# The end phases of an attention + feed-forward kernel: sums of quarters made in PSUM from one PSUM and one SBUF operand, and the seven products' chains in another order

## The chip, the cores and the metric

The kernel runs on one core of a Trainium2 chip. Its engines are named as the profile names them: PE (TensorE, matrix products; PEld is its load of stationary operands), DVE (VectorE), ACT (ScalarE), POOL (GpSimd) and SP (SyncE, which here only issues DMAs). SBUF and PSUM are the two on-chip memories; a matmul writes to PSUM, which has eight banks of 512 fp32 values in each of 128 partitions. The metric is the device time of one execution in microseconds; lower is better.

## The reference

Causal attention by blocks of 64 positions over 8 batches and 8 heads (576 positions, head size 64), then a feed-forward layer over the 4608 resulting rows. The end phases, which the change touches, compute a part of the feed-forward.

```python
scores = scale * np.matmul(q, k.transpose(0, 1, 3, 2))
...
attn = attn / (np.sum(attn, axis=-1, keepdims=True) + 1e-09)
...
x = np.ascontiguousarray(attn_out.transpose(0, 2, 1, 3)).reshape(B * S, H * D)
...
h = x @ w_in                              # 4608 x 512 by 512 x 2048
g = h * (1.0 / (1.0 + np.exp(-h)))
return (g @ w_out).astype(np.float32)     # 4608 x 2048 by 2048 x 512
```

## The kernel before

**Precision.** Each fp32 operand of the feed-forward is kept as two numbers of a format that PE takes at full rate: H, the rounded value, and L, the rest. A product then takes three matmuls (H by H, H by L, L by H). H is made by a copy on ACT, L by a subtraction "source minus H" on DVE or POOL. The helper `parts` (L857) records such a pair, `ops` (L861) records one addition or subtraction, and both end in `tt` (L848), whose only line, L849, stands in the profile for all of them.

**Main part and end phases.** Up to about 906 us the kernel does attention and, interleaved, the feed-forward of 14 of its 18 blocks of 256 rows in the plain way. Blocks 14 to 17 (`LATER`) are left for the end. They form two double blocks of 512 rows, whose rows wait in `x_dram`. Their two matrix products are done with seven products of quarters in place of eight, as Strassen and Winograd do it, which needs sums and differences of quarters of both operands ("q" below), and sums of products at the end.

**Phase b, the first product and silu.** `item` (L975) is one double block by 256 columns of `w_in`: seven products of six matmuls each. Phase b is 16 items: double block 0 with column groups d = 0 to 3, double block 1 with 0 to 3 and 4 to 7, double block 0 with 4 to 7. Products chain in PSUM: bank X takes products 1, 6, 7 and 4, each added to those before it; Z takes 5 and 3; Y takes 2. Between two links of a chain the value so far is copied to SBUF (`keep`, names s1, s2, s5, s3), since it is needed on its own; the next link may start only when that copy has read the bank. `add` makes the four quarters of the item's result from one bank and one kept value (one of the four from two kept values), ACT applies silu, and SP saves the two halves `g0` and `g1` to `g_dram`. There are two buffers of `g0`, one of `g1`.

**Preparations.** `prep_x` (L887) loads the quarters of one double block (tiles `rx`), makes four differences of them in place and splits seven quarters in H and L; it runs three times. `prep_s` (L925) makes the four sums of quarters of a column group of `w_in`, eight times, from a tile `raw` that holds the quarters' H + L again. `prep_t` (L947) does the same for a row group of `w_out`, eight times. `prep_g` (L1068) loads the saved g's quarters and makes their sums and splits, 16 times, for phase c. All differences are made in SBUF from two SBUF operands; the L's are shared out between DVE and POOL.

**Phase c, the second product.** `mult_c` (L1098) is one of four parts (q) of a block of 256 rows: seven products of six matmuls each, 16 calls in all. Each product has half a bank for the whole block; after the fourth part `keep_c`, `add_c` and `store_c` combine the seven and write the result. Successive blocks alternate between two sets of four banks.

**What sets the order.** Each step is put in a list by `at` (L833) with a planned time in us, where 0 is the start of phase b and `ITEM` = 4.94 the planned length of an item; the list is sorted by that time and issued (L1160). Planned times only order the instructions of each engine. Each engine then takes its own in that order and waits at each for what it needs.

Of the kernel before, what the change touches and what calls it, by code (L numbers as in the profile page):

```python
# [20 lines left out]
P = 128  # L21
# [22 lines left out]
USE = (1, 2, 6, 5, 7, 3, 4)  # L44
# [97 lines left out]
def attn_ffn(ctx: ExitStack, tc: tile.TileContext, qk, v, qk0, v0, qk1, v1, w_in, w_out, out):  # L142
# [694 lines left out]
    for i in range(left):  # L837
        at(FULL * (i - left), ffn, 1)
# [7 lines left out]
    right = {}  # L846

# [9 lines left out]
    def parts(t, h, l, src, eng, lag=0.9):  # L857
        at(t, lambda: A.copy(h, src()))
        at(t + lag, lambda: tt(eng, l, src(), h, SUB))

    def ops(t, e, out, a, b, op):  # L861
        at(t, lambda: tt(e, out(), a(), b(), op))

# [23 lines left out]
    def prep_x(t, u):  # L887
        z = {}

        def load(c):  # L890
            raw(z, c, "rx")
            nc.sync.dma_start(out=z[c].rearrange("p (c n) t -> p c (n t)", c=2), in_=x_dram[order[u]][:, 2 * c : 2 * c + 2, :])

        def q(c, n):
            return lambda: z[c].rearrange("p (c n) t -> p c n t", c=2)[:, :, n]

        b11, b12, b21, b22 = q(0, 0), q(0, 1), q(1, 0), q(1, 1)

        def t2():
            if u:  # L900
                z["t"] = right["p"].tile([P, 2, TB], F32, tag="tx", name="tx")
            return z["t"] if u else b22()

        def hl(t, j, src, eng):
            p = pair(u, j)
            if u:
                t = max([t] + [u * span - ITEM + (USE.index(i) + 1) * ITEM / 7 + 0.02 for i in USE if ring[u - 1][i] == ring[u][j]])
            parts(t, p[:, :, 0], p[:, :, 1], src, eng)

        at(t, load, 0)  # L910
        at(t, load, 1)
        hl(t + 4.0, 1, b11, V)
        hl(t + 4.7, 2, b21, G)
        ops(t + 5.6, V, b11, b12, b11, SUB)
        hl(t + 5.4, 3, b22, V)
        ops(t + 6.3, V, b12, b22, b12, SUB)
        ops(t + 7.0, V, t2, b22, b11, SUB)
        two_ = (lambda: z["t"]) if u else b22
        ops(t + 7.7, V, b21, b21, two_, SUB)
        hl(t + 7.7, 6, two_, G)  # L920
        hl(t + 8.4, 5, b11, V)
        hl(t + 9.1, 7, b12, G)
        hl(t + 9.8, 4, b21, V)

    def prep_s(t, d):  # L925
# [3 lines left out]
        h21, l21 = [w[:, 0:2, cols(d, 1)] for w in wi]  # L929
        at(t, raw, z, 0)  # L930

        def q(i, j=None):
            return lambda: z[0].rearrange("p q (c m) -> p q c m", c=2)[:, i : i + 1 if j is None else j]

        def whole(f):
            tt((G, V)[f], z[0][:, 2 * f : 2 * f + 2].rearrange("p q (c m) -> p (q c) m", c=2), f32(wi[0][:, :, cols(d, f)]), f32(wi[1][:, :, cols(d, f)]), ADD)

        at(t, whole, 0)
        at(t, whole, 1)
        ops(t + 0.9, V, q(3), q(2), q(3), ADD)  # L940
        ops(t + 1.4, V, q(2), q(0), q(2), SUB)
        ops(t + 1.8, V, q(0), q(3), q(0), SUB)
        ops(t + 2.3, V, q(1), q(1), q(0), SUB)
        parts(t + 1.4, h21, l21, lambda: q(3)()[:, 0], V, 1.6)
        parts(t + 2.8, H, L, q(0, 3), G)

    def prep_t(t, d):  # L947
# [3 lines left out]
        B = [w[:, 2 * d : 2 * d + 2, :].rearrange("p f (n m) -> p (f n) m", n=2) for w in wo]  # L951
        at(t, raw, z, 0)

        def q(i, j=None):
            return lambda: z[0][:, i : i + 1 if j is None else j]

        at(t, lambda: tt(G, z[0], f32(B[0]), f32(B[1]), ADD))
        ops(t + 2.6, V, q(0), q(1), q(0), SUB)
        ops(t + 3.0, V, q(1), q(3), q(1), SUB)
        ops(t + 3.5, V, q(3), q(3), q(0), SUB)  # L960
        ops(t + 3.9, V, q(2), q(2), q(3), SUB)
        parts(t + 3.5, H[:, 0:2], L[:, 0:2], q(0, 2), V)
        parts(t + 4.4, H[:, 2:4], L[:, 2:4], q(2, 4), G)
# [11 lines left out]
    def item(t, u, d, k):  # L975
        z = {}
        e = d % HALFD
        stat = {
            1: [w[:, 0:2, cols(d, 0)] for w in wi],
            2: [w[:, 2:4, cols(d, 0)] for w in wi],  # L980
            4: [w[:, 2:4, cols(d, 1)] for w in wi],
            5: [w[:, 0:2, cols(d, 1)] for w in wi],
            6: [w[:, e, 0] for w in sv],
            3: [w[:, e, 1] for w in sv],
            7: [w[:, e, 2] for w in sv],
        }

        def prod(i, o):
            if i == 1:
                z["X"] = bank(k % 2)[:, :TB]  # L990
                z["g"] = [both(k) for k in range(2)]
            elif i == 2:
                z["Y"] = bank(2)[:, :TB]
            elif i == 5:
                z["Z"] = pU.tile([P, 512], F32, tag="U", name="Z")[:, :TB]
            x = pair(u, i)
            n = 0
            for c in range(2):
                for a, b in ((0, 0), (0, 1), (1, 0)):
                    nc.tensor.matmul(z[o], stat[i][a][:, c], x[:, c, b, :], start=i in (1, 2, 5) and n == 0, stop=n == 5, skip_group_check=True)  # L1000
                    n += 1

        def keep(e, name, o):
            z[name] = half("s1" if name == "s5" else name)
            (e.copy if e is A else e.tensor_copy)(z[name], z[o])

        def add(e, q, a, b):
            tt(e, z["g"][q[0]][:, q[1]], z[a], z[b], ADD)

        def silu2(h):  # L1010
# [10 lines left out]
        p = ITEM / 7  # L1021
        for n, (i, o) in enumerate(((1, "X"), (2, "Y"), (6, "X"), (5, "Z"), (7, "X"), (3, "Z"), (4, "X"))):
            at(t + n * p, prod, i, o)
        at(t + p + 0.01, keep, A, "s1", "X")
        at(t + 2 * p + 0.01, add, V, (0, 0), "Y", "s1")
        at(t + 2.6 * p, silu2, 0)
# [5 lines left out]
        at(t + 6 * p + 0.45, silu2, 1)  # L1032
        at(t + 7 * p + 0.1, save, 1)
        at(t + 7 * p + 0.15, silu21)
        at(t + 7 * p + 0.5, save, 0)

    at(-0.005, start_b)
    for u in range(nuse):
        if u == 0 or order[u] != order[u - 1]:
            prep_x(u * span - 14.0, u)  # L1040
        for e in range(HALFD):
            d = e + HALFD * (u >= NDBL)
            t = u * span + e * ITEM
            if u in (0, NDBL):
                prep_s(t - 6.5 - (u > 0) * 1.5, d)
            item(t, u, d, u * HALFD + e)
    for d in range(HALFD):
        prep_t(end_b - span - 13.0 + 6.0 * d, d)
        prep_t(end_b - span + 11.0 + 5.5 * d, HALFD + d)

    flat = lambda z: z.rearrange("p a b c -> p (a b c)")
    et = lambda z: z.rearrange("p (j e t) -> p j e t", e=2, t=P)
# [15 lines left out]
    def prep_g(t, blk, q, c, tag):  # L1068
# [12 lines left out]
        def w(i, j=None):  # L1081
            return lambda: z[0].rearrange("p q (e t) -> p q e t", e=2)[:, i : i + 1 if j is None else j]
# [121 lines left out]
```

## Time and profile before

| what | us |
|---|---|
| median of the two runs | 1151.69 |
| the two runs | 1150.3 and 1153.09 |
| the profiled execution, its own time | 1154.32 |
| its span, first to last instruction | 1152.6 |
| PE busy in the span | 1057.3 (92%) |
| DVE busy | 948.2 (82%) |
| POOL busy | 829.2 (72%) |
| ACT busy | 793.9 (69%) |

The profile is of one execution. Its times count from the start of its span, and busy shares are means over parts with different limits. A row of a group of instructions reads: line, engine, operation, output <- inputs by the names in the program, partitions x elements, type, and how many; behind the first bar the busy time in all (us) and the mean of one (ns); behind the second the time that the engine sat idle just before them and what ended most of it ("<-ACT s L1005" is ACT's instruction of line 1005 that wrote s). A row of the timeline gives start (us), length (us), engine, instruction and, in brackets, the idle time before it and what ended it. L1000 is PE in phase b, L1111 PE in phase c.

### The profile page before, as it was taken

The page shows a single profiled execution, that of the slowest core. Times are in us where ns is not written, and L with a number is a line of the kernel's source. Part 1 is how long each engine was busy: PE and PEld are TensorE (multiplying, and loading weights), DVE is VectorE, ACT ScalarE, POOL GpSimd, SP SyncE. Part 2 cuts the span into 40 slices and gives each one's busy share as a digit, 9 for nine tenths or more (in the row PEclk, how much of TensorE's full clock was granted, in tenths as well). Part 3 has the DMA queues.
Part 4 walks back from the last instruction along what each step waited for, and adds up shares of the span by engine and source line. Part 5 has one row for each costly group of instructions (what it writes and reads, how often), then busy time and mean ns, then how long its engine had stood idle before and what let it go on. Part 6 is the DMA issues. An engine that isn't in the chain of part 4 may idle for free.

```text
span 1152.6 us, 21493 instructions
## 1 busy us (share of the span) xinstructions
PE 1057.3 (92%) x7348; PEld 966.5 (84%) x7348; DVE 948.2 (82%) x2513; ACT 793.9 (69%) x1294; POOL 829.2 (72%) x751
## 2 busy tenths in 40 slices
PE   9999999999989997999999779999999787677987
PEld 8888999999978886889989669889889687577887
DVE  7986799999699996999985789999992757879665
ACT  5776688889788877888884768888873454443332
POOL 5766699889969886798976678878773646655344
PEclk9999999999999998999999889999999899788999
DMA  7873333232232321313221222332312033132431
GB/s 272 274 251 107 80 82 82 59 82 59 63 91 49 90 57 41 90 49 92 67 73 45 55 71 66 84 88 58 99 46 64 22 124 107 48 121 66 119 92 56
DMA packets 61389, 102.06 MB, mean 89 GB/s; under 512 B 7264, under 2 KB 34400, under 8 KB 61280
## 3 DMA queue, kind: packets, MB, share of 16 engines
q1 hardware_dynamic: 61280, 100.69, 30.9%
q8 instruction: 58, 0.95, 0.3%
q14 instruction: 51, 0.42, 0.1%
HBM read 80.74 MB, written 19.92 MB: 87 GB/s over the span
## 4 chain that ended last, share of the span: by engine, by line
PE 45%; DVE 28%; issue 8%; ACT 7%; POOL 7%; DMA 4%; SPq 2%; POOLq 0%; DVEq 0%; ACTq 0%
PE h L652 15%; PE o L687 15%; PE U L405 5%; PE S L326 4%; DVE Mx L270 3%; DVE Dx L270 3%; DVE raw L849 3%; PE S L1000 2%; DVE rx L849 2%; DVE m L341 1%; DVE Xm L279 1%; DVE xu L416 1%; ACT p L367 1%; POOL pl L381 1%; DVE MR L274 1%
## 5 line engine op out<-in xcount | busy, mean ns | idle before, releaser
L652 PE MATMUL h<-x,wi 128*128 128x256 f32 x2688 | 349.5, 284 | 0.0
L652 PEld LDWEIGHTS h<-x,wi 128*128 128x128 f32 x2688 | 339.8, 191 | 8.5 <-issue 0.5
L687 PE MATMUL o<-wo,g 128*128 128x512 f32 x1296 | 328.9, 399 | 0.0
L381 POOL TENSOR_TENSOR pl<-p,ph 128x448 fp32r<-128x448 f32 (+1 forms) x192 | 225.7, 1202 | 86.6 <-ACT ph L373 86.5
L687 PEld LDWEIGHTS o<-wo,g 128*128 128x128 f32 x1296 | 238.5, 190 | 48.6 <-issue 0.7
L670 POOL TENSOR_TENSOR g<-g,g 128x512 fp32r<-128x512 f32 x112 | 145.4, 1298 | 57.9 <-ACT g L665 42.7
L270 DVE TRANSPOSE_TENSOR_REDUCE Mx<-S 64x4 f32<-64x128 f32 (+4 forms) x384 | 132.9, 401 | 57.2 <-PE S L326 57.0
L270 DVE TRANSPOSE_TENSOR_REDUCE Dx<-p 128x14 f32<-128x448 f32 (+3 forms) x320 | 122.5, 445 | 0.1
L367 ACT ACTIVATE p<-T 128x512 f32<-128x512 f32 (+1 forms) x192 | 106.9, 605 | 19.7 <-POOL ph L383 14.0
L405 PE MATMUL U<-ph,vc 128*128 128x448 f32 (+3 forms) x320 | 78.8, 312 | 34.4 <-DVE xu L421 22.3
L302 POOL TENSOR_TENSOR qh<-qkraw,qh 64x576 fp32r<-64x576 f32 x64 | 91.7, 1433 | 18.0 <-ACT qh L298 9.1
L373 ACT CAST ph<-p 128x512 fp32r<-128x512 f32 (+1 forms) x192 | 104.0, 596 | 0.7 <-PE U L405 0.5
L659 ACT ACTIVATE g<-h 128x512 f32<-128x512 f32 x112 | 67.0, 598 | 47.4 <-POOL g L670 31.6
L367 ACT ACT_TABLE_LOAD x60 | 77.0, 1283 | 28.1 <-DVE T L356 26.8
L405 PEld LDWEIGHTS U<-ph,vc 128*128 128x128 f32 x320 | 59.1, 196 | 44.0 <-POOL ph L383 27.9
L326 PE MATMUL S<-qh 128*128 128x448 f32 (+3 forms) x320 | 91.1, 297 | 1.0 <-DVE T L356 0.7
L665 ACT CAST g<-g 128x512 fp32r<-128x512 f32 x112 | 69.4, 620 | 22.2 <-PE o L687 20.2
L326 PE MATMUL S<-ql,qh 128*128 128x448 f32 (+3 forms) x320 | 83.8, 306 | 0.0
L659 ACT ACT_TABLE_LOAD x64 | 82.1, 1283 | 1.1
L298 ACT CAST qh<-qkraw 128x1024 fp32r<-128x1024 f32 x64 | 66.8, 1044 | 16.8 <-DMA qkraw<-in_qk_dram 13.4
L304 POOL TENSOR_TENSOR ql<-qkraw,qh 128x448 fp32r<-128x448 f32 x64 | 74.1, 1158 | 5.0
L358 DVE TENSOR_TENSOR T<-S,MR 128x256 f32<-128x256 f32 (+2 forms) x192 | 72.9, 405 | 0.0
(206 smaller groups left out, 1959.5 us busy)
## 6 DMA issues: line engine op xcount, KB each, us to landing
qkraw<-in_qk_dram SPq DMA_DIRECT2D x128, 256.0 KB, 3.9
vraw<-in_v_dram SPq DMA_DIRECT2D x64, 160.0 KB, 3.0
gd<-g SPq DMA_DIRECT2D x32, 256.0 KB, 2.1
wst<-in_moe_w_out_dram SPq DMA_DIRECT2D x15, 512.0 KB, 5.0
rx<-gd SPq DMA_DIRECT2D x44, 128.0 KB, 2.7
wst<-in_moe_w_in_dram SPq DMA_DIRECT2D x10, 512.0 KB, 5.2
out_dram<-ot SPq DMA_DIRECT2D x17, 256.0 KB, 2.9
v<-in_v_dram SPq DMA_DIRECT2D x12, 256.0 KB, 5.9
```

Of the source, the lines that this page charges most:

```text
L270: nc.vector.tensor_reduce(out=out, in_=in_, axis=AX.X, op=op, apply_transpose=True)
L302: nc.gpsimd.tensor_tensor(out=u.qh[64:, NQ:], in0=u.raw[64:, NQ:], in1=u.qh[64:, NQ:], op=ALU.subtract)
L304: nc.gpsimd.tensor_tensor(out=u.ql, in0=u.raw[:, :NQ], in1=u.qh[:, :NQ], op=ALU.subtract)
L326: nc.tensor.matmul(u.ps(c, w, m), u.kk[:, j * P : j * P + m], qq[:, q0 : q0 + w], start=i == 0, stop=i == 1)
L367: nc.scalar.activation(u.p[:, c:e], T[:, c:e], AF.Exp, scale=SCALE)
L373: nc.scalar.copy(u.ph[:, c:e], u.p[:, c:e])
L381: nc.gpsimd.tensor_tensor(out=u.pl[:, c:e], in0=u.p[:, c:e], in1=u.ph[:, c:e], op=ALU.subtract)
L405: nc.tensor.matmul(U[:m, q0 : q0 + w], u.vc[:, j, :m], (u.ph, u.pl)[pp][:, c : c + w], start=n == 0, stop=n == 8)
L652: nc.tensor.matmul(h[:, f, :], wi[wt][:, c, w], x[:, xt, :], start=n == 0, stop=n == 3 * CT - 1)
L659: nc.scalar.activation(g, hs.pop((blk, d)), AF.Silu)
L670: nc.gpsimd.tensor_tensor(out=g2[:, 1], in0=g, in1=g2[:, 0], op=ALU.subtract)
L687: nc.tensor.matmul(o, g2[:, gt, f, tk], wo[wt][:, 2 * d + f, c], start=d == 0 and n == 0, stop=d == NSTEP - 1 and n == 5,)
```

## The change

The sums of quarters are no longer made in SBUF. A new helper `quad` copies one quarter into PSUM with ACT and makes all four sums there, each from one operand in PSUM and one in SBUF; H and L are then made from PSUM, all these L's by DVE. `prep_x` does the same with 512-element quarters. Only L's of unchanged quarters stay on POOL, which also makes both halves of `prep_s`'s `raw`. Banks for these sums come from the two tags (`h` and `o`) that phase c no longer uses, since each of its blocks now takes the same four banks; a small table `held` pushes a preparation's planned time back until its buffers are free by the plan.

In an item the products now come in the order 6, 5, 2, 7, 1, 3, 4, where the 1 is the next item's. s3 is gone: the result that needed it is read from X before product 4 is added. s5 is copied by ACT, and all four adds are on DVE. In phase c the seven products are combined in another pairing, by seven adds on DVE and one copy.

```diff
-USE = (1, 2, 6, 5, 7, 3, 4)
+USE = (1, 6, 5, 2, 7, 3, 4)
...
+    USED = {i: n for n, i in enumerate((6, 5, 2, 7, 1, 3, 4))}
+    p7 = ITEM / 7
...
+    def quad(t, z, q, kind, where, outs):
+        def x(i):
+            return lambda: z["b"][i // 2][:, 256 * (i % 2) : 256 * (i % 2) + 256]
+
+        def start():
+            z["b"] = psum(where)
+            A.copy(x(3)(), q(2 if kind == "S" else 1)())
+
+        t = wait(where, t)
+        hold(where, t + 3.15)
+        at(t, start)
+        if kind == "S":
+            ops(t + 0.5, V, x(0), x(3), q(3), ADD)
+            ops(t + 0.9, V, x(1), q(0), x(3), SUB)
+            ops(t + 1.3, V, x(2), x(0), q(0), SUB)
+            ops(t + 1.7, V, x(3), q(1), x(2), SUB)
...
+        for i, n, h, l, c in outs:
+            parts(t + (2.2 if i > 1 else 1.72) + 0.05 * i, h, l, lambda i=i, n=n, c=c: c(z["b"][i // 2][:, 256 * (i % 2) : 256 * (i % 2) + 256 * n]), V, 0.75)
+        return t + 3.15
...
 def prep_g
-        parts(t + 4.0, H[0][:, 0:2], L[0][:, 0:2], w(0, 2), V)
-        parts(t + 4.1, H[0][:, 2:3], L[0][:, 2:3], w(3), V, 0.7)
-        ops(t + 5.3, V, w(3), w(2), w(3), ADD)
-        ops(t + 5.7, V, w(2), w(0), w(2), SUB)
-        ops(t + 6.1, V, w(0), w(3), w(0), SUB)
-        ops(t + 6.5, V, w(1), w(1), w(0), SUB)
-        parts(t + 6.9, H[1], L[1], w(0, 4), G, 1.2)
+        parts(t + 4.5, H[0][:, 0:2], L[0][:, 0:2], lambda: z[0][:, 0:2], G, 0.7)
+        parts(t + 5.2, H[0][:, 2:3], L[0][:, 2:3], lambda: z[0][:, 3:4], G, 0.7)
+        end = quad(t + 4.0, z, lambda i: lambda: z[0][:, i], "S", where, [(0, 2, H[1][:, 0:2], L[1][:, 0:2], c), (2, 2, H[1][:, 2:4], L[1][:, 2:4], c)])
...
 def item
-        at(t + p + 0.01, keep, A, "s1", "X")
-        at(t + 2 * p + 0.01, add, V, (0, 0), "Y", "s1")
-        at(t + 3 * p + 0.01, keep, A, "s2", "X")
-        at(t + 4 * p + 0.01, keep, V, "s5", "Z")
-        at(t + 5 * p + 0.01, keep, A, "s3", "X")
-        at(t + 5.6 * p, add, G, (1, 1), "s5", "s3")
-        at(t + 6 * p + 0.01, add, V, (1, 0), "Z", "s2")
+            at(t + USED[i] * p7 - ITEM * (i == 1), prod, k, i, o)
+        at(t - 2 * p7 + 0.01, keep, "s1", "X")
+        at(t + p7 + 0.01, keep, "s2", "X")
+        at(t + 2 * p7 + 0.01, keep, "s5", "Z")
+        at(t + 3 * p7 + 0.01, add, 0, 0, "Y", "s1")
+        at(t + 4 * p7 + 0.01, add, 1, 1, "X", "s5")
+        at(t + 6 * p7 + 0.01, add, 1, 0, "Z", "s2")
...
 def mult_c
-            z["b"] = banks_c(z["n"])
+            z["b"] = [bank(0), bank(2), pU.tile([P, 512], F32, tag="U", name="c2"), bank(1)]
```

Of the new `prep_x`, `prep_s` and `prep_t`: `prep_s` and `prep_t` call `quad`, with one 256-element L each for two of the sums of `prep_s` and 512-element L's otherwise; `prep_x` makes its four differences and four L's of them as eight DVE instructions of 512 elements.

The first place is PE at the start of phase b. S is a PSUM bank (the X of one item, or Y), Z the bank of products 5 and 3; `wi`, `sv` hold the stationary operands, `x` and `xown` the moving ones. Before, from the second half of product 1 on:

```order
L1000 MATMUL S_11589<-x,wi_78 128x256 x2
L1000 MATMUL S_11589<-x,wi_79 128x256
L1000 MATMUL S_11599<-x,wi_78 128x256 x2
L1000 MATMUL S_11599<-x,wi_79 128x256
L1000 MATMUL S_11599<-x,wi_78 128x256 x2
L1000 MATMUL S_11599<-x,wi_79 128x256
L1000 MATMUL S_11589<-xown,sv_11387 128x256 x2
L1000 MATMUL S_11589<-xown,sv_11388 128x256
```

One product (2, in S_11599) stands between products 1 and 6 of the chain in S_11589. Now, on PE at the border of the first and second item, from the second half of the second item's product 1 on:

```order
L1054 MATMUL S_11652<-x,wi_78 128x256 x2
L1054 MATMUL S_11652<-x,wi_79 128x256
L1054 MATMUL Z<-x,sv_11387 128x256 x2
L1054 MATMUL Z<-x,sv_11388 128x256
L1054 MATMUL Z<-x,sv_11387 128x256 x2
L1054 MATMUL Z<-x,sv_11388 128x256
L1054 MATMUL S_11594<-x,wi_78 128x256 x2
L1054 MATMUL S_11594<-x,wi_79 128x256
L1054 MATMUL S_11594<-x,wi_78 128x256 x2
L1054 MATMUL S_11594<-x,wi_79 128x256
L1054 MATMUL S_11652<-x,sv_11387 128x256 x2
```

Two products of the item before (3 in Z, 4 in S_11594) now stand between products 1 and 6 in S_11652.

The second place is DVE between the tenth and the eleventh item of phase b, from the tenth's last add. Before (`raw`, `rx`, `tx` are SBUF tiles):

```order
L849 TENSOR_TENSOR g_12237<-Z,s_12281 128x256
L849 TENSOR_TENSOR raw<-raw 128x256 x2
L849 TENSOR_TENSOR wi_79<-raw,wi_78 128x2x128
L849 TENSOR_TENSOR raw<-raw 128x256
L849 TENSOR_TENSOR x<-rx,x 128x2x256
L849 TENSOR_TENSOR raw<-raw 128x256
L849 TENSOR_TENSOR wi_79<-raw,wi_78 128x2x256
L849 TENSOR_TENSOR g_12319<-S_12334,s_12341 128x256
```

Now, with q the sums in PSUM:

```order
L851 TENSOR_TENSOR g_12310<-Z,s_12289 128x256
L851 TENSOR_TENSOR wi_79<-q,wi_78 128x2x128
L851 TENSOR_TENSOR sv_11388<-q,sv_11387 128x256
L851 TENSOR_TENSOR x<-q,x 128x2x256
L851 TENSOR_TENSOR q<-rx,q 128x512
L851 TENSOR_TENSOR sv_11388<-q,sv_11387 128x512
L851 TENSOR_TENSOR q<-q,raw 128x256
L851 TENSOR_TENSOR q<-raw,q 128x256
L851 TENSOR_TENSOR x<-q,x 128x2x256
L851 TENSOR_TENSOR q<-raw,q 128x256
L851 TENSOR_TENSOR g_12401<-S_12384,s_12337 128x256
```

Each instruction now has one operand in PSUM, and nine in place of seven stand between the two adds.

The third place is DVE where phase c begins, from the last item's last add. Before:

```order
L849 TENSOR_TENSOR g_12715<-Z,s_12765 128x256
L849 TENSOR_TENSOR raw<-raw 128x256 x4
L849 TENSOR_TENSOR wi_79<-raw,wi_78 128x2x256
L849 TENSOR_TENSOR x<-rx,x 128x256
L849 TENSOR_TENSOR x<-rx,x 128x512
L849 TENSOR_TENSOR rx<-rx 128x256 x4
L849 TENSOR_TENSOR raw<-raw 128x256 x4
```

Now:

```order
L851 TENSOR_TENSOR g_12803<-Z,s_12777 128x256
L851 TENSOR_TENSOR sv_11387<-q,sv_11388 128x512 x2
L851 TENSOR_TENSOR q<-q,raw 128x256
L851 TENSOR_TENSOR q<-raw,q 128x256 x3
L851 TENSOR_TENSOR q<-q,rx 128x256
L851 TENSOR_TENSOR wi_79<-q,wi_78 128x2x256
L851 TENSOR_TENSOR q<-rx,q 128x256
L851 TENSOR_TENSOR q<-q,rx 128x256
L851 TENSOR_TENSOR wi_79<-q,wi_78 128x2x256
L851 TENSOR_TENSOR q<-rx,q 128x256
L851 TENSOR_TENSOR x<-q,x 128x512 x2
```

All L's of the sums now stand on DVE, among them those that POOL had before; from this add on to the end of the last `prep_t`'s and the fifth `prep_g`'s DVE work there are 38 such instructions without an add of a result between them.

More of the change, by code (lines that the diff above doesn't have):

```diff
@@ L913, in prep_x @@
[L913 to L925, printed above, removed]
+        at(t + 4.0, start)
+        hl(t + 4.2, 1, b11, G)
@@ L926, in prep_s @@
+        for _ in range(2):
+            hold("rx", max(ends) + 0.05)
+    def prep_s(t, d, where):
         z = {}
@@ L973, in both @@
         return right["p"].tile([P, 2, TB], F32, tag=f"g{k}", name=f"g{k}", bufs=2 - k)
[L975 to L988, printed above, removed]
+    items = [{} for _ in range(nuse * HALFD)]
@@ L998, in prod @@
[L998 to L1008, printed above, removed]
@@ L1010, in silu2, with item, keep, add @@
-        def silu2(h):
+        if i in (1, 2, 4, 5):
+            stat = [w[:, (0, 2)[i in (2, 4)] :, cols(d, i > 2)] for w in wi]
+        else:
+            stat = [w[:, e, {7: 0, 6: 1, 3: 2}[i]] for w in sv]
+        x = pair(u, i)
+        n = 0
+        for c in range(2):
+            for a, b in ((0, 0), (0, 1), (1, 0)):
+                nc.tensor.matmul(z[o], stat[a][:, c], x[:, c, b, :], start=i in (1, 2, 5) and n == 0, stop=n == 5, skip_group_check=True)
+                n += 1
+    def item(t, k):
+        z = items[k]
+        u, e = divmod(k, HALFD)
+        d = e + HALFD * (u >= NDBL)
+        def keep(name, o):
+            z[name] = half(name)
+            A.copy(z[name], z[o])
+        def add(h, f, a, b):
+            if "g" not in z:
+                z["g"] = [both(j) for j in range(2)]
+            tt(V, z["g"][h][:, f], z[a], z[b], ADD)
+        def silu_b(h):
@@ L1066, in attn_ffn, with prep_g @@
     blocks = [2 * dbl + h for dbl in order[NDBL:] for h in range(2)]
-    def prep_g(t, blk, q, c, tag):
+    def prep_g(t, blk, q, c, tag, where):
         H, L = c
```

194 lines of the change are left out of this document (110 added, 84 removed).

## Prediction

> **What bounds the kernel now.** I read the 40 slices first, since the change touches the end alone. Of PE's busy tenths and of the TensorE clock's, the last ten of 40 slices are the end phases.
>
> ```profile
> PE   9999999999989997999999779999999787677987
> PEclk9999999999999998999999889999999899788999
> ```
>
> Up to there PE is nearly full; in the end phases it falls to 6 to 8 tenths, and its clock falls too. So something feeds PE too slowly there. Next the start of phase b, and the busy times by stretch (columns: stretch, length; busy time and count of PE, PEld, DVE, ACT, POOL; granted clock; DMA).
>
> ```profile
> 905.98 1.23 PE L1000 MATMUL S<-x,wi 128*128 128x256 f32 x9
> ...
> 906.00:1040.00 134.00, 98.92 (x673) 94.05 (x672) 99.72 (x151) 62.38 (x144) 75.89 (x52) 0.88 0.27 91
> 1040.00:1148.80 108.80, 91.22 (x674) 87.55 (x672) 77.52 (x117) 33.13 (x58) 50.96 (x28) 0.92 0.29 83
> 1148.80:1152.60 3.80, 0.00 (x0) 0.00 (x0) 0.42 (x2) 0.00 (x0) 0.56 (x1) 1.00 0.37 138
> ```
>
> Phase b takes 134.0 us, phase c 108.8, the last store 3.8. What would they take with PE never waiting? The same product, two items apart, in an undisturbed stretch of b, and two successive parts of c:
>
> ```profile
> 947.34 0.89 PE L1000 MATMUL S<-xown,wi 128*128 128x256 f32 x6
> ...
> 957.75 0.88 PE L1000 MATMUL S<-xown,wi 128*128 128x256 f32 x6
> ...
> 1071.98 0.40 PE L1111 MATMUL S<-wo,xown 128*128 128x256 f32 x2
> ...
> 1077.02 1.60 PE L1111 MATMUL S<-wo,sv 128*128 128x256 f32 x12
> ```
>
> An item of b takes (957.75 - 947.34) / 2 = 5.2 us, a part of c 1077.02 - 1071.98 = 5.04. Sixteen of each are 83.3 and 80.6 us. So 134.0 - 83.3 = 50.7 us are lost in b and 108.8 - 80.6 = 28.2 in c, together 78.9. PE's waits (behind the colon: us in all, times, longest) say to whom:
>
> ```profile
> PE S L1000 <- ACT s L1005: 19.4, 13, 5.5
> PE Z L1000 <- DVE s L1005: 15.7, 8, 3.0
> PE c L1111 <- POOL x L849: 5.3, 4, 1.7
> PE S L1111 <- POOL x L849: 4.1, 4, 1.4
> PE c L1111 <- ACT x L858: 2.9, 1, 2.9
> PE c L1111 <- POOL sv L849: 1.8, 1, 1.8
> PE S L1111 <- POOL sv L849: 1.8, 1, 1.8
> PE c L1111 <- POOL wi L849: 0.8, 1, 0.8
> PE c L1111 <- ACT wi L858: 0.7, 1, 0.7
> ```
>
> In b it is 35.1 us for the copies that part the chains (s1, s2, s3 by ACT, s5 by DVE), in c 17.4 us for H's and L's. That is 52.5 of the 78.9. The other 26.4 are matmuls at a lower clock, 0.5 us for each us of waiting. One such wait, on all three engines:
>
> ```profile
> 975.11 2.38 POOL L849 TENSOR_TENSOR raw<-wo,wo 128x1024 f32<-128x1024 f32 x1
> 977.45 1.71 POOL L849 TENSOR_TENSOR raw<-wi,wi 128x512 f32<-128x512 f32 x1
> ...
> 975.18 2.86 DVE L849 TENSOR_TENSOR raw<-wi,wi 128x512 f32<-128x512 f32 x1 [0.42 <-POOL sv L849]
> 978.07 1.37 DVE L849 TENSOR_TENSOR raw<-raw 128x256 f32<-128x256 f32 x1
> 979.36 0.41 DVE L1005 COPY s<-Z 128x256 f32<-128x256 f32 x1
> ...
> 979.83 1.65 PE L1000 MATMUL Z<-xown,sv 128*128 128x256 f32 x6 [3.00 <-DVE s L1005]
> 981.28 1.48 PE L1000 MATMUL S<-xown,wi 128*128 128x256 f32 x6
> ```
>
> DVE's two-operand work starts while POOL's runs and ends just after it (975.18 + 2.86 = 978.04; POOL's ended at 977.49); the next one ends with POOL's next. The copy of s5 stands behind them in DVE's order, PE behind the copy for 3.00 us, and then six matmuls start 1.45 us after the last six where 0.72 is usual. Whether this is a rule is told by lengths (ns, least/median/most):
>
> ```profile
> L849 DVE TENSOR_TENSOR raw<-raw x83: 407/425/2545, 905.1 to 1141.1; 128x256 f32<-128x256 f32 x83
> L849 DVE TENSOR_TENSOR rx<-rx x48: 409/425/2715, 930.9 to 1134.9; 128x256 f32<-128x256 f32 x44, 128x512 f32<-128x512 f32 x4
> L849 DVE TENSOR_TENSOR g<-S,s x18: 410/424/427, 914.8 to 1144.5; 128x256 f32<-128x256 f32 x18
> L849 DVE TENSOR_TENSOR g<-Z,s x16: 408/420/425, 918.9 to 1039.1; 128x256 f32<-128x256 f32 x16
> ```
>
> With both operands in SBUF the same addition takes 407 to 2545 ns; with one in PSUM, in the same stretch beside the same POOL work, 34 times out of 34 at most 427. So DVE's wait for POOL in two-SBUF-operand work is what delays the copies, and DVE's own 99.7 us of 134 in b are in good part such waits.
>
> **The change, part by part.** Prices come from these rows; all exist with the operands where the change puts them.
>
> ```profile
> L247 DVE SCALAR_TENSOR_TENSOR S<-wst,S 128x512 uint32<-128x512 uint32 x21 | 14.6, 694 | 0.6
> L636 DVE TENSOR_TENSOR x<-S,x 128x512 fp32r<-128x512 f32 x4 | 2.7, 687 | 8.8 <-ACT x L633 8.8
> L220 ACT ACTIVATE S<-wst 128x512 f32<-128x512 f32 x4 | 2.6, 640 | 5.4 <-DMA wst<-in_moe_w_in_dram 5.4
> L633 ACT CAST x<-S 128x512 fp32r<-128x512 f32 x4 | 2.4, 599 | 0.4 <-PE S L628 0.4
> L1005 ACT COPY s<-S 128x256 f32<-128x256 f32 x48 | 17.7, 368 | 14.8 <-PE S L1000 14.5
> L849 POOL TENSOR_TENSOR x<-rx,x 128x1024 fp32r<-128x1024 f32 x5 | 11.9, 2380 | 15.6 <-ACT x L858 15.6
> L670 POOL TENSOR_TENSOR g<-g,g 128x512 fp32r<-128x512 f32 x112 | 145.4, 1298 | 57.9 <-ACT g L665 42.7 <-issue 6.1 <-ACT x L450 4.4
> ```
>
> *DVE's load.* A short instruction (256) is 0.42 us, a long one (512) 0.69; a sum written to PSUM from PSUM and SBUF has its row in L247 (0.694), an L from PSUM in L636 (0.687). In the two phases now: 16 items x 3 adds, 48 short = 20.2 us; two `prep_x` of 8 long = 11.0 (the first runs ahead of b under the plain feed-forward's matmuls); about seven `prep_s` of 6 short and 1 long = 22.5 (the first likewise); eight `prep_t` of 4 and 2 = 24.5; 16 `prep_g` of 4 and 2 = 49.0; 28 adds in c = 11.8. Sum 139 us, against 99.7 + 77.5 = 177 before and against 164 us of undisturbed PE: DVE fits, but not by much. A sum in PSUM could be dearer than L247's; if a short one cost as much as a long one, 0.27 us more, DVE would hold 33 us more for the 124 of them, and the crowded places below, with 44 of them, 12 more: with the clock 18, a time of 1112, the upper bound; the lower is nothing. I take nothing, since the row has the same operands.
>
> *ACT* gains one copy for each preparation (32 x 0.37 us) and s5, loses s3: some 118 us of 164, no bound. *POOL* loses all L's of sums and 24 additions of results and gains 8 halves of `raw` at 1.30: off the path, and nothing of DVE's waits for it any more except `raw` itself.
>
> *The chains.* s1, s2 and s5 each now have two or three products (0.74 us each) before the next link, where there was one. A copy takes 0.37, so in an undisturbed item nothing waits; the 35.1 us go, as far as DVE and ACT keep up. The same holds of the adds, which must free X before product 4 and Z before the next 5: two products, 1.5 us.
>
> *Where DVE does not keep up.* Within an item of 5.2 us DVE has room for the adds (1.26) and about one preparation (3.1). By the new order there are four places with more: the second to third item (9 short, 6 long: 7.9 us, 2.7 too many); the tenth, which the second listing shows in part (12 short, 6 long: 9.2, 4.0 too many, and 0.5 in the eleventh); the fifteenth (11 and 4: 7.4, 2.2 too many); and the start of c, where 24 short and 12 long, 18.4 us (third listing), lie ahead of the last row group of `w_out`, which is due at 3 x 5.04 + 2 x 0.72 = 16.6: 1.8 too many. Sum 11.2 us. In the first three 1.5 us each of slack covers a part; against it stand DVE's waits there for ACT's H's, five or six a place, of which I let 1 to 1.5 us a place show. I take the two as equal: 11.2 us of PE waits.
>
> *The single g1.* The second half of an item's result may be written only when the last item's save has landed. The rows for that (the silu of that half, and the least/median/most of a save or load of g):
>
> ```profile
> L1013 ACT ACTIVATE g<-g 128x512 f32<-128x512 f32 x16 | 10.1, 630 | 15.3 <-POOL g L849 11.5 <-DVE g L849 3.8
> ...
> DMA to landing us min/median/max: 2.0/2.4/4.8
> ```
>
> The first add into g1 now follows product 7, the fourth of an item's seven; it was planned at 5.6 sevenths. From it: add 0.42, three sums of a preparation 1.26, second add 0.42, silu 0.63, landing 2.4 and some four handings-over of 0.1 make 5.5 us, 0.3 more than an item; in the eight items with a preparation between the adds, 2.5 us. Bounds: 0 by the shortest landing (2.0), 22 if each took 4.8 (with the clock, 1122). The trace of before lists no wait of that add for a landing; I take 2.5.
>
> *SP.* In c each store stands ahead of one part's loads in SP's order, as before; that part is now the block's fourth, 15 us away, and a landing takes 2.4: nothing. The last store is the same 3.8 us, after one add of 0.42 as before.
>
> **The sum.** 11.2 + 2.5 = 13.7 us of waits, and at 0.5 us of slow clock for each, 20.6 lost in place of 78.9. Start 906.0 + 83.3 + 80.6 + 3.8 + 20.6 = 1094.3 of span. The profiled execution's own time is 1154.32 at a span of 1152.6, 1.7 more: 1096.0. It was 2.6 above the median of 1151.69, so against that: 1093.4, say 1094.
>
> The slow clock is the least sure factor. The row beside 979.83 is one of a short wait:
>
> ```profile
> 1105.16 3.26 PE L1111 MATMUL c<-wi,sv 128*128 128x256 f32 x16 [1.83 <-POOL sv L849]
> ```
>
> Sixteen matmuls take 3.26 us after a wait of 1.83, where 0.12 each is usual; so I keep the factor for waits of one to two us. [...]
>
> [...] The row is 424 ns for g<-S,s beside 425 for raw<-raw: one operand in PSUM costs nothing more. [...]
>
> **The rivals.**
> 1. *PE is the bound throughout*: the slack covers all four places and g1. Span 1073.7, time 1073. For it: DVE's mean load is 85%. Against: places with 40 to 75% more than an item holds.
> 2. *Handings-over*: DVE takes its work in order, and each preparation has three waits for ACT. If each of the 32 stops PE for 0.6 us on top, 19 us, with the clock 29: 1123. For it: PE's longest waits in b are of this kind, through a queue and not through load. Against: most preparations are planned five us ahead of their use.
> 3. *Slower*: the same, but longer each time. The sum leaves 1151.7 - 1093.4 = 58 us of gain, which is 39 us of waits with their slow clock, or 1.2 us for each of the 32: from there on no gain, from 1.7 slower by 2%, and at 2 us 1189. For it: PE stopped up to 5.5 us behind ACT before. Against: ACT itself stood there behind DVE's delayed sums, which now take 0.42.
> 4. *No relief*: DVE waits for POOL also with one operand in PSUM, and the time stays near 1150. Against: 34 of 34 rows.
>
> **How the numbers follow.** Crowded places, 1077 to 1110: 0.60. PE-bound, below 1077: 0.15. Handings-over, 1110 to 1129: 0.16. No relief or a balance within 2%: 0.05. Slower: 0.04. The likeliest gives 1094. The range runs from 1074, just above rival 1's value, to 1126, past rival 2's and the bounds of the two unknown prices (1112, 1122), and leaves out about 0.07 below and 0.12 above. Faster by over 2% (below 1128.7; 2% is about what a measurement of this kernel can tell from no change) holds the first three cases: 0.91; within 2% 0.05; slower 0.04.
>
> **What would show it.** Right: DVE's 256-element sums into PSUM near 0.42 us without long ones; POOL's 512 at 1.30; PE's waits for s below 10 us in b; those left in items 2, 3, 10, 11, 15 and at the fourth part of c, behind DVE's adds or L's of `wi`; the clock near 0.97. Wrong: sums of 0.5 us or more, waits of DVE for a landing of g above 1 us an item, or PE waits in items that hold no preparation.

## The result, and the profile after

| what | before | after |
|---|---|---|
| median, us | 1151.69 | 1094.19 |
| its two runs, us | 1150.3, 1153.09 | 1092.6, 1095.79 |
| the profiled execution, its own time | 1154.32 | 1095.79 |
| its span | 1152.6 | 1094.1 |
| PE busy | 1057.3 (92%) | 1041.4 (95%) |
| DVE busy | 948.2 (82%) | 895.1 (82%) |
| POOL busy | 829.2 (72%) | 779.7 (71%) |
| ACT busy | 793.9 (69%) | 802.5 (73%) |

The ratio is 0.950, 95% interval 0.942 to 0.958. Two more sets of the changed kernel, on other chips beside the kernel before, gave 0.9465 (0.9437 to 0.9493) and 0.9459 (0.9441 to 0.9477), at 1093.27 and 1092.58 us.

The 40 slices of the changed kernel, PE's busy tenths and the granted clock:

```profile
PE   9999999999989999799998977999999998989998
PEclk9999999999999999899999998999999999999999
```

The last ten slices, which stood at 6 to 8 with a slow clock, are nearly full, at a granted clock of 0.98 in phase b and 1.00 in c. Where the end phases begin (timeline of PE: start, length), and the busy times by stretch (phase b, phase c; columns as in the prediction):

```profile
901.34 8.59 PE L687 MATMUL o<-wo,g 128*128 128x512 f32 x36
911.43 0.98 PE L1054 MATMUL S<-x,wi 128*128 128x256 f32 x6 [1.50 <-DVE sv L851]
913.45 0.99 PE L1054 MATMUL S<-x,sv 128*128 128x256 f32 x6 [1.04 <-ACT s L1064]
914.27 1.45 PE L1054 MATMUL Z<-xown,wi 128*128 128x256 f32 x6
915.52 1.48 PE L1054 MATMUL S<-xown,wi 128*128 128x256 f32 x6
916.80 1.28 PE L1054 MATMUL S<-x,sv 128*128 128x256 f32 x6
917.91 0.88 PE L1054 MATMUL S<-x,wi 128*128 128x256 f32 x6
...
909.90:1005.20 95.30, 86.39 (x673) 83.22 (x673) 67.62 (x158) 64.52 (x166) 45.03 (x32) 0.98 0.38 128
1005.20:1090.30 85.10, 82.09 (x674) 80.88 (x672) 59.05 (x132) 38.51 (x87) 32.78 (x31) 1.00 0.37 106
```

The plain feed-forward ends at 901.34 + 8.59 = 909.9, 3.8 us later than before (906.1). Phase b takes 95.3 in place of 133.9, phase c 85.1 in place of 108.7. Against the prediction's undisturbed 83.3 and 80.6 that is 12.0 and 4.5 lost, 16.5 in place of 78.9. One stretch of slow matmuls is left, right behind the first two waits: the products at 914.27, 915.52 and 916.80 need 3.64 us up to the next start where 2.16 is usual, and the granted clock from 914.3 to 917.6 is 0.50. DVE needs 67.6 + 59.1 us for more instructions (158 and 132 for 151 and 117), where it was busy for 177 before. Its groups say why, and POOL's beside them (ns, least/median/most; `q` is a bank of PSUM that holds sums):

```profile
L851 DVE TENSOR_TENSOR q<-raw,q x49: 419/428/430, 909.9 to 1079.5; 128x256 f32<-128x256 f32 x49
L851 DVE TENSOR_TENSOR q<-q,raw x32: 422/432/433, 913.1 to 1079.0; 128x256 f32<-128x256 f32 x32
L851 DVE TENSOR_TENSOR wi<-q,wi x23: 415/681/693, 915.6 to 1023.4; 128x512 fp32r<-128x512 f32 x16, 128x256 fp32r<-128x256 f32 x7
L851 POOL TENSOR_TENSOR raw<-wi,wi x16: 1265/1298/1327, 906.4 to 957.9; 128x512 f32<-128x512 f32 x16
```

No 256-element sum is longer than 433 ns; before, the same sums reached 2545. POOL's 512 take 1.30, as expected. PE's waits from 890 us on:

```profile
PE S L1054 <- DVE g L851: 3.1, 3, 1.3
PE S L1054 <- ACT s L1064: 2.7, 3, 1.1
PE S L1160 <- DVE g L851: 1.5, 3, 1.0
PE S L1054 <- DVE sv L851: 1.5, 1, 1.5
PE Z L1054 <- DVE g L851: 1.4, 3, 1.0
PE S L1160 <- DVE wi L851: 0.9, 1, 0.9
PE S L1160 <- ACT wi L867: 0.6, 1, 0.6
```

Together 11.7 us where there were 52.5, none above 1.5. Their places besides the two at the start of b (three waits of 0.17 to 0.25 are left out, and two rows around the wait at 969.02 are put in for use below):

```profile
928.49 0.98 PE L1054 MATMUL S<-x,sv 128*128 128x256 f32 x6 [0.59 <-ACT s L1064]
...
967.18 0.88 PE L1054 MATMUL S<-x,sv 128*128 128x256 f32 x6
969.02 0.98 PE L1054 MATMUL Z<-x,wi 128*128 128x256 f32 x6 [0.96 <-DVE g L851]
969.83 0.88 PE L1054 MATMUL S<-x,wi 128*128 128x256 f32 x6
...
974.39 0.97 PE L1054 MATMUL S<-xown,wi 128*128 128x256 f32 x6 [1.32 <-DVE g L851]
...
980.76 0.97 PE L1054 MATMUL S<-xown,wi 128*128 128x256 f32 x6 [0.86 <-DVE g L851]
...
982.88 0.98 PE L1054 MATMUL Z<-x,wi 128*128 128x256 f32 x6 [0.24 <-DVE g L851]
...
1001.74 0.98 PE L1054 MATMUL S<-x,sv 128*128 128x256 f32 x6 [1.07 <-ACT s L1064]
...
1004.42 0.98 PE L1054 MATMUL S<-x,wi 128*128 128x256 f32 x6 [0.94 <-DVE g L851]
...
1022.91 0.38 PE L1160 MATMUL S<-wi,x 128*128 128x256 f32 x1 [0.60 <-ACT wi L867]
1024.15 1.21 PE L1160 MATMUL S<-wi,x 128*128 128x256 f32 x8 [0.86 <-DVE wi L851]
...
1029.99 0.50 PE L1160 MATMUL S<-wi,xown 128*128 128x256 f32 x2 [1.04 <-DVE g L851]
```

Behind each of these waits in phase b the six matmuls take 0.97 or 0.98, only 0.1 more than without a wait.

### The profile page after: what moved, and what is told of

It is laid out like the page before. It is cut to its first block, busy times and chain, and to the rows that moved or that the text cites. A ratio compares the mean times of both kernels' runs of the same rounds, so it can differ in the third digit from the quotient of the medians.

```text
span 1094.1 us, 21551 instructions
## 1 busy us (share of the span) xinstructions
PE 1041.4 (95%) x7348; PEld 953.6 (87%) x7348; DVE 895.1 (82%) x2537; ACT 802.5 (73%) x1349; POOL 779.7 (71%) x735
## 5 line engine op out<-in xcount | busy, mean ns | idle before, releaser
L652 PEld LDWEIGHTS h<-x,wi 128*128 128x128 f32 x2688 | 343.5, 193 | 8.6 <-issue 0.5
```

The source lines that it names most:

```text
L652: nc.tensor.matmul(h[:, f, :], wi[wt][:, c, w], x[:, xt, :], start=n == 0, stop=n == 3 * CT - 1)
```

## The experiments

Theory P: DVE work with two SBUF operands waits for POOL, and the change gains by giving each sum one operand in PSUM. Rival O: the new order of the products makes the gain. Other questions came up on the way. The table orders the kernels by what they share with the change; b and c are lengths of the profiled execution, b from the end of the last 36 matmuls of the plain feed-forward (start + 8.59) to the first matmul of c, c from there to the end of the last matmul (start + 0.88). A ratio is that of the runs to runs of the kernel before on the same chip.

| kernel | 36 matmuls start | c starts | last matmul starts | b, us | c, us | ratio (95%) |
|---|---|---|---|---|---|---|
| before | 897.55 | 1040.07 | 1147.88 | 133.9 | 108.7 | 1 |
| e3: new order alone | 897.67 | 1027.69 | 1136.02 | 121.4 | 109.2 | 0.992 (0.990 to 0.994) |
| e7_x_in_psum: and x in PSUM | 897.03 | 1021.88 | 1129.63 | 116.3 | 108.6 | 0.986 (0.983 to 0.989) |
| e1c_shares: all but PSUM sums, old shares | 897.92 | 1014.34 | 1119.13 | 107.8 | 105.7 | 0.975 (0.974 to 0.977) |
| e1b: all but PSUM sums | 897.74 | 1016.00 | 1113.18 | 109.7 | 98.1 | 0.970 (0.968 to 0.973) |
| e1a: half the sums from two SBUF operands | 899.09 | 1008.93 | 1097.70 | 101.2 | 89.7 | 0.957 (0.954 to 0.959) |
| e2: all but the order | 898.51 | 1008.21 | 1092.59 | 101.1 | 85.3 | 0.952 (0.950 to 0.954) |
| e0_changed: as changed | 899.39 | 1002.58 | 1086.77 | 94.6 | 85.1 | 0.9465 (0.944 to 0.949) |

**Half of the sums from two SBUF operands.** In `quad` of the changed kernel:

```diff
-            A.copy(x(3)(), q(2 if kind == "S" else 1)())
...
-            ops(t + 0.5, V, x(0), x(3), q(3), ADD)
-            ops(t + 0.9, V, x(1), q(0), x(3), SUB)
+            ops(t + 0.5, V, x(0), q(2), q(3), ADD)
+            ops(t + 0.9, V, x(1), q(0), q(2), SUB)
```

> The changed kernel, but two of the four sums of each preparation of W_in, W_out and g take both operands from SBUF again (their results stay in PSUM); the copy of a quarter into PSUM by ACT, which is then not needed, is left out. Theory P (DVE work with two SBUF operands waits for POOL's work): these two of four sums (some 64 instructions) show lengths up to 1.3 or 2.4 us beside POOL's instructions, the other sums stay at 0.42 to 0.44; 10 to 25 us slower than the changed kernel, 1104 to 1120. Rival O (it is the new order of the products that gained, where the operands lie does not matter): all sums near 0.42, 1091 to 1096.

Measured 1104.22 us (1103.38 to 1108.08), more than the changed kernel by 1.0% of the time before (0.9568 to 0.9465), some 12 us. DVE's groups, first the sums with two SBUF operands, then those with one, in the same stretch beside the same POOL work:

```profile
L851 DVE TENSOR_TENSOR q<-raw x40: 417/434/2323, 911.2 to 1086.5; 128x256 f32<-128x256 f32 x40
L851 DVE TENSOR_TENSOR q<-raw,q x29: 412/428/430, 908.9 to 1088.5; 128x256 f32<-128x256 f32 x29
```

Of the sums with two SBUF operands, those of g from `rx` (`q<-rx`, 22) even have a median of 842. The place of the operands decides whether DVE waits (up to 2323 ns beside at most 430); a result in PSUM does not spare it, since both groups write PSUM. It costs although the instruction that it saves, ACT's copy, is gone.

**All of these sums in SBUF.** The four sums of W_in, W_out and g in place from two SBUF operands. With that go three smaller things: the L's of these sums read two SBUF operands too, ACT's copy is left out, and g's sums start 1.5 us later by plan. The rest is as changed:

```diff
-            ops(t + 0.5, V, x(0), x(3), q(3), ADD)
+            ops(t + 0.5, V, q(3), q(2), q(3), ADD)
```

> The changed kernel, but the four sums of each preparation of W_in, W_out and g are made in place in SBUF from two SBUF operands as before the change, without ACT's copy into PSUM; the order of products, the share of POOL and the preparation of x stay as changed (the L's of g's sums start 1.5 us later by plan). Theory P: most of the gain is lost, 1115 to 1140, with PE waits behind DVE's adds. Rival O: at most 1100.

Measured 1120.81 us (1118.62 to 1122.21), more than the changed kernel by 2.4% of the time before (0.9703 to 0.9465). b and c are 15 and 13 us longer. So P holds: the operands' place, with these three things, is worth nearly half of the 5.4%. The rest was not P's, and the next kernels looked for it.

**All but the order, and the order alone.** The first is the changed kernel with the old order within an item, the second the kernel before with the new one. In the second the low part of one of x's seven quarters is made from the quarter after its subtraction, so its values differ; number, kind and length of the instructions don't.

```diff
-USE = (1, 6, 5, 2, 7, 3, 4)
+USE = (1, 2, 6, 5, 7, 3, 4)
```

> The changed kernel with the order of products, copies and adds within an item of phase b as before the change (one add on POOL, s5 copied by DVE, s3 kept); sums in PSUM as changed. Theory P (the sums' operands made most of the gain): 1100 to 1115, PE waits of 0.3 to 0.5 us for s in each item. Rival O (the order made it): 1125 to 1150.

Measured 1099.54 us (1098.41 to 1101.2), just below the range. PE's waits for the copies are back, fewer and longer than the 0.3 to 0.5 us in each item that were expected (us in all, times, longest):

```profile
PE S L1058 <- ACT s L1063: 11.2, 11, 1.9
```

> The kernel before with the new order of products, copies and adds within an item of phase b (all adds on DVE, s5 copied by ACT); the preparations stay in SBUF as before. Theory P: DVE still waits for POOL, so the waits are only shortened by the new slack of one or two products; 1120 to 1145. Rival O: at most 1105.

Measured 1145.09 us (1142.44 to 1146.01), at the upper end. In the profiled executions the order alone gives b 12.5 us (133.9 to 121.4), c nothing (by the ratio of the runs it is some 9.5 us); on top of the PSUM sums it gives 6.5 (101.1 to 94.6). Rival O falls, but the order is no trifle: the room of two products swallows what DVE is late by, and the later DVE is, the more it is worth. P expected e3 to lose its remaining time to DVE, and its longest group of PE's waits in b is for DVE's adds:

```profile
PE S L998 <- DVE g L851: 15.9, 7, 3.6
```

**More work on POOL.** A direct test of P: 48 POOL additions in phase b that nothing uses, three in each item, in the changed kernel and in e1b.

```diff
+        def more():
+            tt(G, right["dump"], f32(wo[0][:, 0, 0:256]), f32(wo[1][:, 0, 0:256]), ADD)
+
+        for n in range(3):
+            at(t + 1.2 + 1.65 * n, more)
```

> The changed kernel with three more POOL additions of 128x256 in each item of phase b, read from W_out in SBUF and used by nothing: 48 of some 0.73 us, 35 us of POOL. Theory P (DVE work with one operand in PSUM does not wait for POOL): DVE's sums stay at 0.42 to 0.43, at most 0.44; time within 3 us of the changed kernel, as far as POOL's own raw is not late. Rival (DVE just has less to do or POOL less to disturb it with): sums of 0.5 to 1.1 us, 10 us or more slower.

> The kernel with the sums made in SBUF (e1b, 0.9703 of before) with the same 48 POOL additions. Theory P: DVE's sums of two SBUF operands wait for them, 0.4 to 0.7 us each time they meet; 8 to 25 us slower than e1b. Rival: as much slower as e5 is than the changed kernel.

With PSUM operands the time stays: 1092.86 (1091.26 to 1093.43) beside 1093.27 for the changed kernel on the same chip, and the sums don't see the additions:

```profile
L851 DVE TENSOR_TENSOR q<-raw,q x49: 419/428/430, 907.9 to 1077.1; 128x256 f32<-128x256 f32 x49
L851 POOL TENSOR_TENSOR dump<-wo,wo x48: 723/742/761, 913.1 to 1002.8; 128x256 bf16<-128x256 f32 x48
```

With SBUF operands it is 1131.25 (1130.51 to 1134.09) for 1120.81 on another chip, 0.980 for 0.970 of the kernel before; phase b goes from 109.7 to 1027.57 - 897.48 - 8.59 = 121.5. DVE's sums in phase b, first of e1b, then of e6_pool_more_sbuf, have twice the median:

```profile
L851 DVE TENSOR_TENSOR raw<-raw x51: 406/424/2565, 905.8 to 1011.6; 128x256 f32<-128x256 f32 x51
```

```profile
L851 DVE TENSOR_TENSOR raw<-raw x51: 409/843/2468, 905.5 to 1022.6; 128x256 f32<-128x256 f32 x51
```

DVE is busy for 97.6 us of phase b there, 86.0 in e1b, which is about the 12 us by which b is longer. POOL's additions wait too:

```profile
L851 POOL TENSOR_TENSOR dump<-wo,wo x48: 728/789/1170, 913.4 to 1027.2; 128x256 bf16<-128x256 f32 x48
```

The same 36 us of POOL work cost nothing in one kernel and 12 us of phase b in the other, and the lengths on both engines tell that in the second each waits for the other (medians of 843 ns on DVE for 424 in e1b, 789 on POOL for 742 in e5_pool_more).

**Who makes the L's.** From e3 to e1b lay 25 us. e1c_shares is e1b with the old shares of DVE and POOL:

```diff
-        end = quad(t + 2.6, z, q, "T", "o", [(0, 2, H[:, 0:2], L[:, 0:2], c), (2, 2, H[:, 2:4], L[:, 2:4], c)])
+        end = quad(t + 2.6, z, q, "T", "o", [(0, 2, H[:, 0:2], L[:, 0:2], c, V), (2, 2, H[:, 2:4], L[:, 2:4], c, G)])
```

> The kernel e1b (sums in SBUF, new order of products) with the split of work between DVE and POOL as before the change as well: the L's of the sums of g, of half of W_out's and of sv on POOL, the L's of g's unchanged quarters and one half of each raw of W_in on DVE. From e3 (only the order new, 0.9918 of before) to e1b (0.9703) lie 2.1%, some 25 us. Theory M (POOL, which itself is held up by DVE's work with two SBUF operands, delivers its L's late): most of that comes back, 1135 to 1146, with 8 us or more of PE waits for x and sv of POOL in phase c. Rival (the preparation of x in PSUM and the new pairing in c made it): at most 1126.

A miss: 1126.62 us (1125.81 to 1127.12). The shares carry 0.5%, some 6 us, not most of the 25. The loss is in c, as theory M had it (98.1 to 105.7, while b is 1.9 shorter), but of PE's waits for POOL's x only this came back there (beside 1.3 us for its L's of `wi` and `sv`; e1b has no wait for POOL in c):

```profile
PE S L1153 <- POOL x L851: 2.8, 2, 1.4
```

**x's differences in PSUM.** e3 with the changed `prep_x`:

```diff
-        ops(t + 5.6, V, b11, b12, b11, SUB)
-        ops(t + 6.3, V, b12, b22, b12, SUB)
+        at(t + 4.0, start)
+        ops(t + 4.7, V, b(0), b(1), b11, SUB)
+        ops(t + 5.4, V, b(1), b22, b(1), SUB)
```

> The kernel e3 (before with the new order of products) with the preparation of x as changed: its four differences of 512 made in PSUM from one PSUM and one SBUF operand, its L's of unchanged quarters on POOL, 2 us earlier by plan; all other sums in SBUF as before. Of the 18 us between e3 (0.9918 of before) and e1c_shares (0.9752), whose cause is open: if x's differences carry them, 1128 to 1136 and the waits about 975, 985 to 995 and 912 shorter; if the plan of the other preparations and phase c carry them, 1141 to 1147.

Measured 1138.08 us (1136.07 to 1138.88), between the two: 0.6% or 7 us of the 18. PE's first long wait in b, in e3 and in e7_x_in_psum:

```profile
912.40 0.79 PE L998 MATMUL S<-x,sv 128*128 128x256 f32 x2 [5.43 <-ACT s L1008]
```

```profile
909.82 0.50 PE L1024 MATMUL S<-x,sv 128*128 128x256 f32 x2 [3.49 <-ACT s L1034]
```

This one became shorter; the other two named, at 975 and 995 in e3, stayed (3.08 and 3.43 us there, 3.10 and 3.60 in e7_x_in_psum). The rest, 8.5 us of b and 2.9 of c between e7_x_in_psum and e1c_shares, came with what the two still differ in: the planned times of the other preparations and phase c's pairing, adds and banks. No run parts these.

**The crowded places.** The changed kernel with its preparations spread by plan. In the first version the preparation of x overwrote quarters that the plain feed-forward still had to read, so that PE waited for them and the values differ; in the second it stands where it was:

```diff
-                preps.append((t - 9.0 - (u > 0) * 1.0, prep_s, e + HALFD * (u > 0), "0U" if u == e == 0 else "h" if (u, e) == (0, 1) else "o"))
+                preps.append((t - (17.0 if u else 11.5 if e == 0 else 9.0), prep_s, e + HALFD * (u > 0), "0U" if u == e == 0 else "h" if (u, e) == (0, 1) else "o"))
...
-        preps.append((end_b - span - 13.0 + 6.0 * d, prep_t, d))
-        preps.append((end_b - span + 11.0 + 5.5 * d, prep_t, HALFD + d))
+        preps.append((end_b - span - 15.0 + 5.5 * d, prep_t, d))
+        preps.append((end_b - span + 6.0 + 5.2 * d, prep_t, HALFD + d))
```

> The changed kernel itself, beside the kernel before on the same chip: 1094 to 1099 by its ratio of 0.95, as a mark for the others.

> The changed kernel with its preparations spread otherwise by plan: the first preparation of x 3 us earlier, the first of W_in 2.5, the later four of W_in 8, those of W_out 2 to 7 earlier. If what is left of the waits comes from places with too much work on DVE (the 2.5 us at the start of b, 3.4 in items 10 to 12, 2.2 in 15 and 16, 1.5 in the fourth part of c), 4 to 8 us faster than the changed kernel and those waits gone. Rival (they are handings-over between ACT and DVE, which move along with the work): no change, within 2 us, waits elsewhere.

> The changed kernel with its preparations spread as in e4_spread, but the first preparation of x where the changed kernel has it. Crowded places: 5 to 7 us faster than the changed kernel, 1086 to 1089 beside 1093, with no PE wait at the end of the plain feed-forward and none above 1.3 us behind. Rival (e4_spread's gain came from the early x): 1091 to 1094.

> The changed kernel again, as the mark for e4b_spread on this chip: 1091 to 1097, 0.944 to 0.95 of before.

The changed kernel itself came out just under its range in the first set (1093.27) and within it in the second (1092.58). e4_spread took 1089.09 us (1088.21 to 1090.89) beside 1093.27 (1092.76 to 1094.96); e4b_spread 1089.54 (1088.82 to 1090.07) beside 1092.58 (1090.96 to 1095.61) on its chip. All four runs of e4b_spread lie below all five of the changed kernel, 3.0 us by the medians: less than the 5 to 7 expected. Its waits at the places in question:

```profile
911.07 0.98 PE L1054 MATMUL S<-x,sv 128*128 128x256 f32 x6 [1.81 <-ACT s L1064]
...
967.23 0.98 PE L1054 MATMUL Z<-x,wi 128*128 128x256 f32 x6 [1.05 <-DVE g L851]
974.90 0.98 PE L1054 MATMUL S<-x,sv 128*128 128x256 f32 x6 [0.53 <-ACT s L1064]
...
997.99 0.98 PE L1054 MATMUL S<-x,sv 128*128 128x256 f32 x6 [1.22 <-ACT s L1064]
```

Those of the fourth part of c are gone, and those between 966 and 983 fell from 0.96 + 1.32 + 0.86 + 0.24 = 3.4 to 1.05 + 0.53: these were load. At the start of b the wait for the bank that the first sums lend (1.50) is gone, but that for the copy s1 grew from 1.04 to 1.81, and the one near 998 stayed: by that these are handings-over. PE's waits in all fell from 12.1 us (e0b_changed) to 8.4. So both theories hold in part, load for about a third. e4b_spread is the fastest version that still computes the same result, 0.943 of before (0.942 to 0.944).

## Why the prediction came out

The time, 1094 for 1094.19, is nearer than its steps deserve: the sum of losses was 4 us too large, and the start 4 us too early. That they cancel so well is luck; that the gain is near 58 us is not, since the waits that were to go went.

*The cause* held: DVE's two-operand work waited for POOL, one operand in PSUM ends that (e1a: at most 430 ns for 2323; e5: 430 beside 48 more POOL additions; e6: a median of 843 with both in SBUF). But it was taken for all of the 58 us. By e1b the place of the operands of W_in's, W_out's and g's sums is worth 2.4% of the 5.4; x's differences add some 0.6% (e7), and the order, the shares and the plan the rest. That POOL is now off the path held, no wait of PE is for it; but moving its L's of sums to DVE is a gain of its own that the prediction did not price, some 6 us with the sums in SBUF (e1c_shares).

*Prices.* Short sums 0.428 and 0.432 for the 0.42 taken, long ones 0.68 for 0.69. "I take nothing" for an operand or a result in PSUM was right to 0.01 us. DVE's 139 us in the end phases were 67.6 + 59.1 = 126.7 of busy time, since lengths were added up and successive instructions overlap; at the start of b two that are 0.42 long start 0.34 us apart:

```profile
910.62 0.42 DVE L851 TENSOR_TENSOR wi<-S,wi 128x256 fp32r<-128x256 f32 x1 [0.25 <-ACT sv L867]
910.96 0.42 DVE L851 TENSOR_TENSOR sv<-S,sv 128x256 fp32r<-128x256 f32 x1
```

*The undisturbed PE.* The 5.2 us of an item were taken from the old order and do not hold for the new one. The same product two items in a row, in a stretch without waits:

```profile
960.33 0.88 PE L1054 MATMUL Z<-xown,sv 128*128 128x256 f32 x6
...
965.37 0.88 PE L1054 MATMUL Z<-xown,sv 128*128 128x256 f32 x6
```

It is 5.04, as in a part of c: 80.6 us for 16 items and not 83.3. Against 80.6 and 80.6 the changed kernel's 95.3 and 85.1 have lost 19.1 us. 11.7 are the waits and 1.5 the slow stretch at the start of b. Each listed wait also costs some 0.25 us more than its length, which makes 3.8 for the 15: behind the product at 967.18 the next usually starts 0.72 later, at 967.90, and so 1.12 before 969.02, but the listed wait of 0.96 counts from the row's end (967.18 + 0.88); and from 969.02 to the next start it is 0.81, not 0.72. The 2.1 that are left are delays too small for the list.

*The crowded places* were to give 11.2 us of waits. PE waited 11.7 in all, but not all of it where it was put (items counted by the add that PE waits for). Tenth to twelfth item: 3.4 for 4.5. Fifteenth and sixteenth: 1.07 + 0.94 = 2.0 for 2.2. Fourth part of c: 1.5 for 1.8. Second to third item: 0.6 for 2.7, so there the slack was real. Not foreseen: the start of b, 1.50 + 1.04, since the first sums of W_in lie in the bank that product 1 needs, and 1.04 at the first border of blocks in c.

*The single g1* cost two waits of DVE, 1.7 us, for the 2.5 taken; PE's own list has no wait for a landing:

```profile
DVE g L851 <- DMA gd<-g: 1.7, 2, 1.0
```

*The slow clock* is the step whose mechanism failed, though its size nearly came out: "0.5 us of slow clock for each" us of waiting, 6.9 in the sum. The runs show 1.5, in one place: behind 1.50 and 1.04 us at the start of b. Behind the other 13 waits the matmuls run at full speed (in phase b six take 0.97 or 0.98 us for 0.88 without a wait), and in e0_changed, whose first wait is 1.49, they do so at the start of b too:

```profile
911.50 0.98 PE L1054 MATMUL S<-x,sv 128*128 128x256 f32 x6 [1.05 <-ACT s L1064]
912.32 0.88 PE L1054 MATMUL Z<-xown,wi 128*128 128x256 f32 x6
```

What filled the place of the rest are the 3.8 us around the waits and the 2.1 of small delays; the granted clock was 0.984 where 0.97 was named. The factor was misread in the same way: of the 26.4 us beside the waits in the kernel before, 34 waits at 0.25 make 8.5, and some 16 are slow matmuls (168 that start 0.213 us apart in place of 0.12). It also was a mean over waits of up to 5.5 us, and the row that was to carry it to short waits (1105.16, 1.83 us) was one of several: in the same listing two waits of 1.8 us were followed by slow matmuls, three of 1.05, 1.42 and 1.69 were not. e3 has the very same wait at full speed (16 matmuls in 2.18 us):

```profile
1093.59 2.18 PE L1114 MATMUL c<-wi,sv 128*128 128x256 f32 x16 [1.83 <-POOL sv L851]
```

*The start*, 906.0, was the other error: in this execution the unchanged part before the end phases took 3.9 us longer (909.9; 907.6 to 908.0 in e0_changed, e0b_changed and e5_pool_more). So the span from there on was 184.2 us for the 188.3 that the sum has, and the two errors cancel.

*The rivals.* PE-bound throughout (1073): no, 11.7 us of waits are left, though e4b_spread shows that some can go. Handings-over of 0.6 us for each of 32 preparations: no; waits for ACT's s are 2.7 us in all. Slower, no relief: no.

## What to carry to other kernels

Where two engines may hold each other up, look at the spread of one instruction's length (407 to 2545 ns for one shape) and not at its mean: the spread tells of waiting inside the instruction, which no list of waits shows, and the same operation with another operand place tells what it depends on: with one in PSUM it was at most 433 ns. A change that gives a late engine both less work and more room gains by each, so parts must be tried alone and left out alone; the order was worth 12.5 us of phase b while DVE was late and 6.5 when it was not. And a price that one row gives should be asked of all rows of its kind: three of the same view spoke against slow matmuls behind each short wait.

## What the runs showed of the hardware

When the clock falls is a matter of more than the length of a wait. A wait of e1b and what follows:

```profile
972.74 0.98 PE L1047 MATMUL Z<-x,wi 128*128 128x256 f32 x6 [1.72 <-DVE g L851]
973.55 0.88 PE L1047 MATMUL S<-x,wi 128*128 128x256 f32 x6
```

After 1.72 us the next product is at full speed (0.81 us to the next start, 0.72 from there on); after 3.00 us, in the prediction's rows at 979.83, matmuls are at half (1.45 us to the next start, a granted clock of 0.50 from 979.8 to 982.5). Two other cases went either way: 1.83 us was followed by slow matmuls in the kernel before (16 in 3.26 us) and by fast ones in e3 (16 in 2.18), and 1.50 and 1.04 us close together by 3.3 us at a granted clock of 0.50 in the changed kernel's first profile, but by none in e0_changed, e0b_changed and e5_pool_more (1.49 and 1.05 us there). What decides it is not shown.

The part ahead of the end phases is the same code in all these kernels, but its last attention addition (`xu<-xu,U`, L421 on DVE) came at 873.9 us in the kernel before and at 875.8 in the changed one of e0_changed, and in eight profiles of kernels with sums of W_in, W_out and g in PSUM between 874.9 and 877.7, in six without between 873.4 and 874.3. Its length is the same, 620 or 621 ns by the median. What makes these one to four us was not tried and stays open.
